# Half-height last passes, in pairs of tiles, in the first feed-forward contraction of an adaLN block

## The chip, the cores and the metric

The kernel runs on 1 core of one Trainium2 chip. The metric is device time in microseconds (us) of that core: a program's time from start to end, as the median of its runs. Beside it stands one profiled execution, from which every duration below is read.

## What is computed

One transformer block on 2048 tokens of width 448 with adaptive layer norm, in float32: sliding-window attention (16 heads, window 256), then a dense feed-forward part of width 1792 with the Mish activation. Cut to what matters here:

```python
mod = (silu(c) @ w_mod).reshape(1, 6, 1, -1)
sa, ca, ga, sb, cb, gb = (mod[:, i] for i in range(6))
h = layernorm(x) * (1 + ca) + sa
x = x + ga * attention(h, wqkv, wo)
h = layernorm(x) * (1 + cb) + sb
h = einsum("bsd,df->bsf", h, w1) + b1        # the first contraction: 448 -> 1792
act = h * tanh(softplus(h))                  # Mish
x = x + gb * einsum("bsf,fd->bsd", act, w2)  # the second contraction: 1792 -> 448
```

## The kernel before

Tokens are worked through in 4 groups g of 512. Every float32 matrix operand is split into a high and a low part, both of type float32r: a product is then high x high + high x low + low x high, three passes over each piece of 128 rows of the contraction. The contraction length 448 is three pieces of 128 rows and one of 64. For the piece of 64 the tiles hold the data twice, in rows 0 to 63 and again in rows 64 to 127: the activations' high and low parts (`hh`, `hl`) are doubled as they are, and of the weights (`w13[:, 3]`) rows 0 to 63 hold the high part and rows 64 to 127 the low part. So one pass of 128 rows gives high x high and high x low together, and a second one with `hl` gives low x high and, beside it, low x low, which is not needed. That makes 11 passes (`passes`, L183; low x high of the last piece is the eleventh). All of them are matmuls of 128 rows.

The feed-forward part has NF = 14 tiles f of 128 hidden features for each group, numbered through as n = 14 g + f, 0 to 55. For a tile n:

- `f1_mm(n)` (L812) puts 11 passes of 512 columns into one PSUM bank z (two such banks, taken in turn).
- `f1_act(n)` (L822): ACT makes Mish of z into `t` (L826, one buffer) and from it the high part `ah` (L827, two buffers); DVE takes the low part `al` (L828, two buffers) as the difference.
- `ff2(n)` (L992): 12 passes of 448 columns, three for each of the 4 token tiles t, added up over f in 4 PSUM banks `acc` (four buffers, so the next group takes the same four banks). At f = 13 DVE reads each bank (L1005, `yo`), adds the residual (L1008), and SP stores the result. The `yo` tiles have three buffers.

The order is written out by hand, and each engine works through its own queue in that order. The main loop (L1035) does, for n: `f1_mm(n)`, `f1_act(n)`, in the first group `pieces(n)` (L792: splits `w2` of tile n, ACT L789 and POOL L790, and for n below 6 two pieces of `w1`, L164 and L170 or L172), a `fill_step`, `ff2(n - 1)`, and one or two more `fill_step`s. So PE has alternating 11 passes z and 12 passes acc: while ACT and DVE work on tile n, PE does `ff2(n - 1)`. A fill step issues a bit of other work: in group 0 the end of the attention part for the last group (`ot`, `wo`), and in groups 0 to 2 the layer norm and the transposes (`trf`, L232, with `hT_hi` L239 on ACT and `hT_lo` L236 and L243 on DVE) for the next group.

Tiles 0 and 1 are done already at the end of the attention loop, by the table `TAIL` (L835): tile 0 in two parts, the load of the activation table for Mish, `f1_act(0)`, tile 1 in two parts, `f1_act(1)`. `ff2(0)` follows in the main loop.

`w1_lo` (L709, through `split_lo` L168) makes the weights' low parts, for the last piece as one operation on rows 64 to 127.

Of the kernel before, what the change touches and what calls it, by code (L numbers as in the profile page):

```python
# [8 lines left out]
F32 = mybir.dt.float32  # L9
# [3 lines left out]
ALU = mybir.AluOpType  # L13

S, D, F, H, DH, W = 2048, 448, 1792, 16, 28, 256
NG, GT = 4, 512
NF = F // 128
# [34 lines left out]
def adaln_block(ctx: ExitStack, tc: tile.TileContext, x, wqkv, wo, w1, b1, w2, c, w_mod, out):  # L52
    nc = tc.nc
    PE, ACT, DVE, POOL = nc.tensor, nc.scalar, nc.vector, nc.gpsimd
# [3 lines left out]
    def dma(o, i):  # L58
        nc.sync.dma_start(o, i)
# [25 lines left out]
    def bank(tag, bufs, name):  # L85
        return PS[0].tile([128, 512], F32, name=name, tag=tag, bufs=bufs)
# [81 lines left out]
    def split_lo(piece, hi, lo, ci, eng):  # L168
        if ci < 3:
            eng.tensor_tensor(lo, piece, hi.bitcast(F32), op=ALU.subtract)  # L170
        else:
            eng.tensor_tensor(hi[64:128], piece[64:128], hi[64:128].bitcast(F32), op=ALU.subtract)  # L172
# [10 lines left out]
    def passes(xh, xl, wh, wl):  # L183
        r = []
        for ci in range(3):
            r += [(xh[:, ci], wh[:, ci]), (xh[:, ci], wl[:, ci]), (xl[:, ci], wh[:, ci])]
        return r + [(xh[:, 3], wh[:, 3]), (xl[:, 3], wh[:, 3])]
# [191 lines left out]
    c0, c1 = QCOLS[0]  # L379
    for ci in range(4):  # L380
        hi = wq3[:, ci, c0:c1]
# [60 lines left out]
    def xr_tile(name):  # L442
        return mid.tile([128, 512], F32, name=name, tag="xr", bufs=3)
# [237 lines left out]
    FW = {}  # L681
    w2h, w2l, w2p, h2, x1 = {}, {}, {}, {}, {}
# [16 lines left out]
    w1p = {}  # L699
# [5 lines left out]
    def w1_hi(n):  # L705
        ci, c0 = W1[n]
        split_hi(w1p[n], FW["w13"][:, ci, c0:c0 + D], ACT)

    def w1_lo(n, eng):  # L709
        ci, c0 = W1[n]  # L710
        split_lo(w1p[n], FW["w13"][:, ci, c0:c0 + D], FW["w1l"][:, min(ci, 2), c0:c0 + D], ci, eng)


    SEQ = [e for f in range(NF) for e in [("w2", f)] + [("w1", n) for n in (2 * f + 4, 2 * f + 5) if n < len(W1)]]
# [1 line left out]
    def piece_load(i):  # L716
        if i < len(SEQ):
            (w2_dma if SEQ[i][0] == "w2" else w1_load)(SEQ[i][1])

    def gen_w1():  # L720
# [23 lines left out]
        for n in range(4):  # L744
            yield
            w1_hi(n)
            yield "dve"
            w1_lo(n, DVE)
# [34 lines left out]
    def w2_split(f):  # L783
        n = NF - 1 - f
        pl = FW["p1"] if f == 0 else FW["ff"]
        w2h[f] = (mid.tile([128, D], F32R, name=f"w2h{f}", tag="wo", bufs=7) if n < 7 else
                  pl.tile([128, D], F32R, name=f"w2h{f}"))
        w2l[f] = pl.tile([128, D], F32R, name=f"w2l{f}")
        ACT.activation(w2h[f], w2p[f], AF.Copy)  # L789
        (DVE if f < 1 else POOL).tensor_tensor(w2l[f], w2p[f], w2h[f].bitcast(F32), op=ALU.subtract)  # L790

    def pieces(f):  # L792
        for i, (kind, n) in enumerate(SEQ):
            if kind == "w2" and n == f:
                w2_split(n)
            elif kind == "w1" and (n - 4) // 2 == f:
                w1_hi(n)
                w1_lo(n, DVE if f < 1 else POOL)
            else:
                continue  # L800
            if "ff" in FW:
                piece_load(i + 6)

    NN = NG * NF
    ah, al, acc = {}, {}, {}

    def ftile(nm, n, dt=F32):
        return FW["p1"].tile([128, GT], dt, name=f"{nm}{n}", tag=nm, bufs=1 if nm == "t" else 2)

    zb = {}  # L810

    def f1_mm(n, tag, part=(0, 11)):  # L812
        g, f = divmod(n, NF)
        hh, hl = h2[g]
        fs = slice(f * 128, (f + 1) * 128)
        if part[0] == 0:
            zb[n] = bank(tag, 2, f"z{n}")
        ps = passes(hh, hl, FW["w13"][:, :, fs], FW["w1l"][:, :, fs])
        for m in range(*part):
            PE.matmul(zb[n], ps[m][1], ps[m][0], start=(m == 0), stop=(m == 10))  # L820

    def f1_act(n):  # L822
        f = n % NF
        ah[n], al[n] = ftile("ah", n, F32R), ftile("al", n, F32R)
        t = ftile("t", n)
        ACT.activation(t, zb[n], AF.Mish, bias=FW["b1c"][:, f:f + 1])  # L826
        ACT.activation(ah[n], t, AF.Copy)  # L827
        DVE.tensor_tensor(al[n], t, ah[n].bitcast(F32), op=ALU.subtract)  # L828

    def mish_table():  # L830
        ACT.add_instruction(mybir.InstLoadActFuncSet(
            act_func_set_id=25, name=nc.get_next_instruction_name(),
            engine=mybir.EngineType.Activation, ins=[], outs=[]))

    TAIL = {  # L835
        0: lambda: (f1_mm(0, "mm", (0, 6)), pieces(0)),
        1: lambda: (f1_mm(0, "mm", (6, 11)), mish_table(), f1_act(0)),
        2: lambda: f1_mm(1, "mm", (0, 6)),
        3: lambda: (f1_mm(1, "mm", (6, 11)), f1_act(1)),
    }  # L840

    VT = ("v0", "v1", "v2", "v3")
# [87 lines left out]
    for u in range(NU + 9):  # L930
        s, k = divmod(u, 3)
        g = s // H
# [12 lines left out]
        a = s + LEAD  # L945
# [46 lines left out]
    def ff2(n):  # L992
        g, f = divmod(n, NF)
        if f == 0:
            acc[g] = [bank("acc", 4, f"acc{g}_{t}") for t in range(4)]
        for t in range(4):
            ts = slice(t * 128, (t + 1) * 128)
            p = acc[g][t][:, 0:D]
            PE.matmul(p, ah[n][:, ts], w2h[f], start=(f == 0), stop=False)  # L999
            PE.matmul(p, ah[n][:, ts], w2l[f], start=False, stop=False)  # L1000
            PE.matmul(p, al[n][:, ts], w2h[f], start=False, stop=(f == NF - 1))  # L1001
            if f == NF - 1:
                j = 4 * g + t
                y = xr_tile(f"yo{j}")[:, 0:D]
                DVE.tensor_tensor(y, p, gbn, op=ALU.mult)  # L1005
                for eng, a, b in (((DVE, 0, D),) if g < NG - 1 else ((POOL, 0, D),) if t < 3 else
                                  ((DVE, 0, 256), (POOL, 256, D))):
                    eng.tensor_tensor(y[:, a:b], y[:, a:b], x1[g][:, t, a:b], op=ALU.add)  # L1008
                dma(of[j * 128:(j + 1) * 128, :], y)

    def gen_x1_ln2(g):
        if g > 1:
            x1_load(g, (ff, p1)[g % 2])
            yield
            yield
            yield

        def xn_tiles():
            t = mid.tile([128, 4, 512], F32, name=f"xn2_{g}", tag="on")
            return [t[:, i] for i in range(4)]  # L1020
        yield from gen_ln2(g, ff, xn_tiles, "tr", 2)
# [8 lines left out]
    def fill_step():  # L1030
        if fill is not None:
            pipe.step()
            next(fill, None)
            flush()
    for n in range(NN + 1):  # L1035
        g, f = divmod(n, NF)
        if f == 0 and n:
            while fill is not None and next(fill, "END") != "END":
                pipe.step()
            fill = None  # L1040
            while pipe.items:
                pipe.step()
        if f == 2 and 0 < g < NG - 1:
            fill = gen_x1_ln2(g + 1)
        if 2 <= n < NN:
            f1_mm(n, "z")
            f1_act(n)
        if 0 < n < NF:
            pieces(n)
        if n:  # L1050
            fill_step()
            ff2(n - 1)
            for _ in range(1 + (g == 0)):
                fill_step()
    for st in (ff_s, mid_s, cst_s, FW["s"], psf_s):
# [24 lines left out]
```

## Time and profile before

| what | value |
| --- | --- |
| runs, median of 3 | 728.78 us (727.68 to 729.99) |
| profiled execution, span from its first to its last instruction | 727.2 us |
| PE matmul busy | 690.9 us, 95% of the span, 3969 instructions |
| VectorE (DVE) busy | 381.4 us, 52% |
| ScalarE (ACT) busy | 392.3 us, 54% |
| GpSimd (POOL) busy | 331.2 us, 46% |
| granted TensorE clock, mean | 0.989 |
| first contraction, matmuls z (L820) | 224 + 224 + 168 |
| second contraction, matmuls acc (L999 to L1001) | 224 each |

The profile gives no time of the profiled execution beside its span; the span is 1.6 us below the median of the runs. The feed-forward part runs from about 422 us to the end. A matmul's duration in the records is from its start to its modelled end; matmuls overlap in the engine, so what a pass costs a full queue is the distance from its start to the next one's start. PEld are the weight loads, which normally run beside the matmul ahead of them. In a row of the timeline stand start, duration, engine, line, operation, output <- inputs, and in brackets how long the engine sat idle before it and what ended that.

### The profile page before, as it was taken

The page shows a single profiled execution, that of the slowest core. Times are in us where ns is not written, and L with a number is a line of the kernel's source. Part 1 is how long each engine was busy: PE and PEld are TensorE (multiplying, and loading weights), DVE is VectorE, ACT ScalarE, POOL GpSimd, SP SyncE. Part 2 cuts the span into 40 slices and gives each one's busy share as a digit, 9 for nine tenths or more (in the row PEclk, how much of TensorE's full clock was granted, in tenths as well). Part 3 has the DMA queues.
Part 4 walks back from the last instruction along what each step waited for, and adds up shares of the span by engine and source line. Part 5 has one row for each costly group of instructions (what it writes and reads, how often), then busy time and mean ns, then how long its engine had stood idle before and what let it go on. Part 6 is the DMA issues. An engine that isn't in the chain of part 4 may idle for free.

```text
span 727.2 us, 11903 instructions
## 1 busy us (share of the span) xinstructions
PE 690.9 (95%) x3969; PEld 588.4 (81%) x3969; DVE 381.4 (52%) x1011; ACT 392.3 (54%) x740; POOL 331.2 (46%) x362
## 2 busy tenths in 40 slices
PE   3989989999999999999999899999999999999996
PEld 2767768888889888888887688888888888888885
DVE  4768645687765688655668942334333223322112
ACT  3516777676776667766878984344223222322221
POOL 4725697676666586766778955322010000000002
PEclk9898999999999999999999999999999999999999
DMA  8776564174483354471666175300300020001001
GB/s 201 213 239 190 186 200 135 56 234 130 123 260 132 115 173 147 137 217 56 182 202 191 48 239 166 115 13 1 102 0 1 1 101 1 1 1 51 1 0 51
DMA packets 48121, 83.86 MB, mean 115 GB/s; under 512 B 6126, under 2 KB 26108, under 8 KB 48060
## 3 DMA queue, kind: packets, MB, share of 16 engines
q1 hardware_dynamic: 48060, 83.10, 37.6%
q8 instruction: 32, 0.52, 0.3%
q14 instruction: 29, 0.24, 0.1%
HBM read 53.45 MB, written 29.36 MB: 114 GB/s over the span
## 4 chain that ended last, share of the span: by engine, by line
PE 69%; issue 11%; DVE 8%; ACT 5%; DMA 4%; POOL 2%; SPq 1%; POOLq 0%; DVEq 0%; ACTq 0%
PE z L820 15%; PE pv L642 8%; PE qk L294 7%; PE qk_v L294 5%; PE acc L1000 5%; PE acc L1001 5%; PE acc L999 5%; PE sA L580 4%; PE wo L294 4%; PE sB L610 4%; PE sB L621 3%; DVE junk L582 3%; ACT P L624 2%; PE et L653 1%; DMA wm<-in_w_mod_dram 1%
## 5 line engine op out<-in xcount | busy, mean ns | idle before, releaser
L632 POOL TENSOR_TENSOR Pl<-P,Ph 128x512 fp32r<-128x512 f32 (+2 forms) x192 | 232.9, 1221 | 80.9 <-ACT Ph L625 47.8
L582 DVE CUSTOM_DVE_ANT_0 junk<-sA,mask 128x384 f32<-128x384 f32 (+2 forms) x256 | 135.3, 529 | 100.7 <-PE sA L580 95.4
L828 DVE TENSOR_TENSOR al<-t,ah 128x512 fp32r<-128x512 f32 x56 | 38.8, 692 | 200.9 <-ACT ah L827 200.9
L624 ACT ACTIVATE P<-sB 128x512 f32<-128x512 f32 (+2 forms) x192 | 109.7, 571 | 63.0 <-PE sB L621 56.2
L826 ACT ACTIVATE t<-z,b1c 128x512 f32<-128x512 f32 x56 | 38.5, 688 | 188.6 <-PE z L820 177.7
L625 ACT ACTIVATE Ph<-sB 128x512 fp32r<-128x512 f32 (+2 forms) x192 | 109.3, 569 | 0.0
L580 PE MATMUL sA<-k,q 84*128 84x384 f32 (+2 forms) x256 | 101.0, 399 | 5.7 <-DVE mx L582 5.2
L820 PE MATMUL z<-hhf,w 128*128 128x512 f32 x224 | 89.5, 400 | 0.0
L820 PE MATMUL z<-hlf,w 128*128 128x512 f32 x224 | 88.8, 396 | 0.0
L999 PE MATMUL acc<-w2h,ah 128*128 128x448 f32 x224 | 82.1, 367 | 0.0
L1000 PE MATMUL acc<-w2l,ah 128*128 128x448 f32 x224 | 82.1, 367 | 0.0
L1001 PE MATMUL acc<-w2h,al 128*128 128x448 f32 x224 | 82.0, 366 | 0.0
L642 PE MATMUL pv<-Pl,v 128*60 128x256 f32 (+2 forms) x352 | 74.2, 285 | 5.1 <-POOL Pl L632 5.0
L642 PE MATMUL pv<-Ph,v 128*60 128x256 f32 (+2 forms) x352 | 76.9, 292 | 2.2 <-ACT o L647 2.0
L610 PE MATMUL sB<-q,k 86*128 86x256 f32 (+1 forms) x352 | 75.1, 287 | 0.4 <-DMA q<-mr 0.2
L820 PE MATMUL z<-hhf,w1l 128*128 128x512 f32 x168 | 66.3, 395 | 0.0
L610 PEld LDWEIGHTS sB<-q,k 86*128 86x128 f32 x352 | 62.2, 191 | 2.3 <-DMA q<-mr 0.6
L621 PE MATMUL sB<-fdmask,identr 128*128 128x128 bf16 (+1 forms) x320 | 60.5, 255 | 0.0
L580 PEld LDWEIGHTS sA<-k,q 84*128 84x128 f32 x256 | 49.3, 194 | 12.9 <-DVE mx L582 11.1
L642 PEld LDWEIGHTS pv<-Ph,v 128*60 128x60 f32 x352 | 45.5, 133 | 16.4 <-ACT o L647 4.3
L642 PEld LDWEIGHTS pv<-Pl,v 128*60 128x60 f32 x352 | 44.9, 132 | 16.2 <-POOL Pl L632 9.6
L1008 POOL TENSOR_TENSOR yo<-yo,x 128x448 f32<-128x448 f32 (+1 forms) x4 | 4.2, 1060 | 108.6 <-DVE yo L1005 108.6
(150 smaller groups left out, 1290.6 us busy)
## 6 DMA issues: line engine op xcount, KB each, us to landing
scr<-st SPq DMA_DIRECT2D x24, 512.0 KB
k<-scr SPq DMA_DIRECT2D x48, 252.0 KB
q<-scr SPq DMA_DIRECT2D x64, 168.0 KB
scr<-st SPq DMA_DIRECT2D x32, 256.0 KB
x<-x1d SPq DMA_DIRECT2D x10, 448.0 KB
xin<-in_A_x_dram SPq DMA_DIRECT2D x8, 448.0 KB
xr<-in_A_x_dram SPq DMA_DIRECT2D x16, 224.0 KB
x1d<-xr SPq DMA_DIRECT2D x16, 224.0 KB
```

Of the source, the lines that this page charges most:

```text
L294: PE.matmul(p, b, a, start=(n == 0), stop=(n == 10))
L580: PE.matmul(p[:, c0:384], q[0:84, t * 128:(t + 1) * 128], k[0:84, t * 128 + c0:t * 128 + 384], start=True, stop=True)
L582: DVE.tensor_tensor_reduce(out=junk[:, c0:384], in0=p[:, c0:384], in1=mask[:, c0:384], scale=1.0, scalar=-3.0e38, op0=ALU.add, op1=ALU.max ...
L610: PE.matmul(p[:, c:c + 128 * (t1 - t0)], k[:, jj * 128:(jj + 1) * 128], q[:, t0 * 128:t1 * 128], start=(n == 0), stop=False, skip_group_ch ...
L624: ACT.activation(P[:, c0:], p[:, c0:], AF.Exp, scale=SCALE)
L625: ACT.activation(Ph[u][:, c0:], p[:, c0:], AF.Exp, scale=SCALE)
L632: eng.tensor_tensor(Pl[u][:, a:b], Pt[u][:, a:b], Ph[u][:, a:b].bitcast(F32), op=ALU.subtract)
L642: PE.matmul(pv[0:60, t0 * 128:t1 * 128], V[j % NV][:, h, :], P[u][:, c:c + 128 * (t1 - t0)], start=(P is Ph and b == 0 and n == 0), stop=F ...
L820: PE.matmul(zb[n], ps[m][1], ps[m][0], start=(m == 0), stop=(m == 10))
L999: PE.matmul(p, ah[n][:, ts], w2h[f], start=(f == 0), stop=False)
L1000: PE.matmul(p, ah[n][:, ts], w2l[f], start=False, stop=False)
L1001: PE.matmul(p, al[n][:, ts], w2h[f], start=False, stop=(f == NF - 1))
```

## The change

The last pass of each z tile (low x high of the 64-row piece) becomes a matmul of 64 rows: rows 0 to 63 for even f, rows 64 to 127 for odd f. So that an odd tile finds the weights' high part in rows 64 to 127, `w1_lo` now puts the low part into rows 0 to 63 for odd f, in pieces of at most 128 columns: four operations in place of one for each of the four last-piece blocks of `w1`.

Tiles go in pairs (n even): ten passes for n, ten for n + 1, then both half-height passes one behind the other (`f1_end`), then `f1_act(n)`. `f1_act(n + 1)` comes behind `ff2(n - 1)`. At odd n the loop now holds `pieces(n)`, fill steps and `ff2(n - 1)` alone. In `TAIL` tile 0 is no longer finished by itself: both halves and both `f1_act` stand at its end.

```diff
     def w1_lo(n, eng):
         ci, c0 = W1[n]
-        split_lo(w1p[n], FW["w13"][:, ci, c0:c0 + D], FW["w1l"][:, min(ci, 2), c0:c0 + D], ci, eng)
+        if ci < 3:
+            split_lo(w1p[n], FW["w13"][:, ci, c0:c0 + D], FW["w1l"][:, ci, c0:c0 + D], ci, eng)
+            return
+        a = c0
+        while a < c0 + D:
+            f = a // 128
+            b = min((f + 1) * 128, c0 + D)
+            r = slice(64, 128) if f % 2 == 0 else slice(0, 64)
+            hi = FW["w13"][r, 3, a:b]
+            eng.tensor_tensor(hi, w1p[n][r, a - c0:b - c0], hi.bitcast(F32), op=ALU.subtract)
+            a = b
...
-    def f1_mm(n, tag, part=(0, 11)):
+    def f1_mm(n, tag, part=(0, 10)):
...
-            PE.matmul(zb[n], ps[m][1], ps[m][0], start=(m == 0), stop=(m == 10))
+            PE.matmul(zb[n], ps[m][1], ps[m][0], start=(m == 0), stop=False)
+
+    def f1_end(n):
+        for i in (n, n + 1):
+            g, f = divmod(i, NF)
+            r = slice(64 * (f % 2), 64 * (f % 2) + 64)
+            PE.matmul(zb[i], FW["w13"][r, 3, f * 128:(f + 1) * 128], h2[g][1][r, 3], start=False, stop=True)
...
     TAIL = {
-        0: lambda: (f1_mm(0, "mm", (0, 6)), pieces(0)),
-        1: lambda: (f1_mm(0, "mm", (6, 11)), mish_table(), f1_act(0)),
-        2: lambda: f1_mm(1, "mm", (0, 6)),
-        3: lambda: (f1_mm(1, "mm", (6, 11)), f1_act(1)),
+        0: lambda: (f1_mm(0, "mm", (0, 5)), pieces(0)),
+        1: lambda: (f1_mm(0, "mm", (5, 10)), mish_table()),
+        2: lambda: f1_mm(1, "mm", (0, 5)),
+        3: lambda: (f1_mm(1, "mm", (5, 10)), f1_end(0), f1_act(0), f1_act(1)),
     }
...
-        if 2 <= n < NN:
+        if 2 <= n < NN and n % 2 == 0:
             f1_mm(n, "z")
+            f1_mm(n + 1, "z")
+            f1_end(n)
             f1_act(n)
         if 0 < n < NF:
             pieces(n)
         if n:
             fill_step()
             ff2(n - 1)
+            if 2 <= n < NN and n % 2 == 0:
+                f1_act(n + 1)
```

Three places show what moves. PE, the end of tile 14's z passes and the start of `ff2(13)`, before (`hhf1`, `hlf1` are the high and low part of group 1's input, `w13` the weights' high part, `ah13` and `al13` the parts of tile 13's activations):

```order
L820 MATMUL z14_6791<-hhf1_6587,w1l_5223 128x512
L820 MATMUL z14_6791<-hlf1_6588,w13_5222 128x512
L820 MATMUL z14_6791<-hhf1_6587,w13_5222 128x512
L820 MATMUL z14_6791<-hlf1_6588,w13_5222 128x512
L999 MATMUL acc0_0_6180<-w2h13_6773,ah13_6767 128x448
```

and the same place in the change:

```order
L830 MATMUL z15_6814<-hlf1_6618,w13_5222 128x512
L830 MATMUL z15_6814<-hhf1_6617,w13_5222 128x512
L836 MATMUL z14_6803<-hlf1_6618,w13_5222 128x512
L836 MATMUL z15_6814<-hlf1_6618,w13_5222 128x512
L1015 MATMUL acc0_0_6186<-w2h13_6785,ah13_6773 128x448
```

Ahead of `ff2(13)` now stand both tiles 14 and 15, and the two half-height passes (L836) follow each other between a pass of 128 rows and the next pass of 128 rows.

PE, a little further, where group 0's last `ff2` ends and group 1's first begins, before (`acc0_3` is the fourth accumulator of group 0, `acc1_0` the first of group 1, in the bank that `acc0_0` had):

```order
L999 MATMUL acc0_3_6183<-w2h13_6773,ah13_6767 128x448
L1000 MATMUL acc0_3_6183<-w2l13_6774,ah13_6767 128x448
L1001 MATMUL acc0_3_6183<-w2h13_6773,al13_6768 128x448
L820 MATMUL z15_6837<-hhf1_6587,w13_5222 128x512
L820 MATMUL z15_6837<-hhf1_6587,w1l_5223 128x512
L820 MATMUL z15_6837<-hlf1_6588,w13_5222 128x512
```

and in the change:

```order
L1015 MATMUL acc0_3_6189<-w2h13_6785,ah13_6773 128x448
L1016 MATMUL acc0_3_6189<-w2l13_6786,ah13_6773 128x448
L1017 MATMUL acc0_3_6189<-w2h13_6785,al13_6774 128x448
L1015 MATMUL acc1_0_6867<-w2h0_6067,ah14_6827 128x448
L1016 MATMUL acc1_0_6867<-w2l0_6068,ah14_6827 128x448
L1017 MATMUL acc1_0_6867<-w2h0_6067,al14_6828 128x448
```

The 11 passes of z15 that stood between the two `ff2` are gone from there. DVE's queue at this place holds `al14`, then the four pairs of `yo` operations, then `al15`, before and now.

ACT, at the end of the attention loop, before (`o2_1` is the last head's output out of PSUM, `ol31` a step of the last pair of heads):

```order
L831 ACT_TABLE_LOAD
L826 ACTIVATE t0_6089<-z0_6058,b1c_5469 128x512
L827 ACTIVATE ah0_6087<-t0_6089 128x512
L647 ACTIVATE o2_1_367<-pv63_6048 60x512
L826 ACTIVATE t1_6112<-z1_6098,b1c_5469 128x512
L827 ACTIVATE ah1_6110<-t1_6112 128x512
L658 ACTIVATE ol31_6121<-et31_6116 128x224
```

and in the change:

```order
L847 ACT_TABLE_LOAD
L647 ACTIVATE o2_1_367<-pv63_6051 60x512
L842 ACTIVATE t0_6109<-z0_6061,b1c_5469 128x512
L843 ACTIVATE ah0_6107<-t0_6109 128x512
L842 ACTIVATE t1_6115<-z1_6094,b1c_5469 128x512
L843 ACTIVATE ah1_6113<-t1_6115 128x512
L658 ACTIVATE ol31_6124<-et31_6119 128x224
```

Tile 0's activation now stands behind the last head's output and directly ahead of tile 1's.

## Prediction

> **What bounds the kernel now.** First the page, then the stretches of the feed-forward part, then single rows.
>
> ```profile
> PE 690.9 (95%) x3969; PEld 588.4 (81%) x3969; DVE 381.4 (52%) x1011; ACT 392.3 (54%) x740; POOL 331.2 (46%) x362
> ```
>
> ```profile
> 600.00:650.00 50.00, 50.00 (x239) 43.17 (x238) 14.40 (x22) 14.55 (x22) 1.14 (x4) 1.00 0.00 1
> ```
>
> The second line is a stretch of 50 us in the feed-forward part: PE (first figure behind the length) is busy for all 50.00, DVE and ACT for 14.4 and 14.55, at full granted clock. Here PE alone sets the time, and a pass less in its queue is worth the distance from one pass to the next. Rows of PE in that stretch, for one tile:
>
> ```profile
> 600.72 0.39 PE L820 MATMUL z<-hhf,w 128*128 128x512 f32 x1
> ...
> 603.05 0.40 PE L820 MATMUL z<-hlf,w 128*128 128x512 f32 x1
> 603.29 0.37 PE L999 MATMUL acc<-w2h,ah 128*128 128x448 f32 x1
> ...
> 605.77 0.39 PE L820 MATMUL z<-hhf,w 128*128 128x512 f32 x1
> ```
>
> The first row is the first of 11 passes z, the second the last: ten steps take 2.33 us, a pass 0.233 us (not the 0.39 of its record). The 12 passes acc take 605.77 - 603.29 = 2.48 us, 0.207 each. Durations come from one execution with a span of 727.2 us; the median of the runs, 728.78, lies 1.6 above it. What the change adds inside the span is added to the median.
>
> **The two half-height passes.** There are 28 pairs. Before, their two passes cost 2 x 0.233 = 0.466 us. If both halves run at once and nothing else happens, a pair saves 0.233, in all 6.5 us: the end below nothing. What speaks for more than that is how PE changes between shapes of tile. One kind of change the trace has hundreds of times, to fewer columns (128*60 in the rows) and back:
>
> ```profile
> 300.22 0.39 PE L294 MATMUL qk<-hh,wql 128*128 128x512 f32 x1
> 300.45 0.40 PE L642 MATMUL pv<-Ph,v 128*60 128x256 f32 x2
> 300.68 0.40 PE L642 MATMUL pv<-Pl,v 128*60 128x256 f32 x2
> 300.92 0.40 PE L610 MATMUL sB<-q,k 86*128 86x256 f32 x2
> ```
>
> The starts lie 0.23 apart throughout, 512 columns each: changing columns costs nothing. Fewer rows occur once, in the transpose b1t with 14 rows (L741):
>
> ```profile
> 384.12 0.18 DVE L193 BATCH_NORM_AGGREGATE mv<-stw 128x2 f32<-128x6 f32 x1
> 384.27 0.36 PE L294 MATMUL wo<-wo,hho 128*128 128x448 f32 x1
> 384.56 0.13 PEld L741 LDWEIGHTS b1t<-ident,b1r 14*128 14x128 f32 x1 [0.31 <-DVE mv L193]
> 384.72 0.18 PEld L642 LDWEIGHTS pv<-Ph,v 128*60 128x60 f32 x2
> 385.00 0.40 PE L642 MATMUL pv<-Pl,v 128*60 128x256 f32 x2
> ```
>
> Its weight load waits for DVE, which ends at 384.30, and starts 0.26 later. What a wait for DVE costs otherwise shows an ordinary load of 128 rows:
>
> ```profile
> 243.94 0.69 DVE L317 TENSOR_TENSOR st<-qk,st 128x512 fp32r<-128x512 f32 x1
> 244.69 0.19 PEld L294 LDWEIGHTS qk<-hh,wq 128*128 128x128 f32 x1 [0.59 <-DVE st L317]
> 244.79 0.19 PEld L294 LDWEIGHTS qk<-hh,wql 128*128 128x128 f32 x1
> 245.03 0.40 PE L294 MATMUL qk<-hh,wql 128*128 128x512 f32 x1
> ```
>
> DVE ends at 244.63, the load starts 0.06 later. So b1t's load is held 0.20 longer, until 0.08 after the pass of wo has run out (384.27 + 0.207 = 384.48). And a load that nothing hides costs 0.10: the next one starts 0.10 behind it, and the two passes lie 0.34 apart in place of 0.23. Behind b1t, the first of the two pv(Ph) passes must have begun 0.23 before 385.00, at 384.77. From the end of wo's pass to there are 0.29 us, for a pass of 14 columns: that is the round trip into fewer rows and back.
>
> The pair in the same way: 0.29 for the round trip, 0.05 more because the load behind it has 128 columns and not 60 (an estimate, half of the 0.10), 0.10 for the second half's own load, 0.23 for the columns of both at once: 0.67 against 0.466, so +0.20 a pair and +5.7 us for 28. Upper end: the halves run one after the other, 0.29 + 0.05 + 0.47 = 0.81, +9.6 us. I take +5.7 because b1t is the only row with fewer rows, and its load visibly did not start beside the pass ahead of it.
>
> [...]
>
> **The new order at the change of groups.** ff2(14) takes the four accumulator banks of ff2(13). Before, the 11 passes of z15 stand between them; now ff2(14) follows at once. This is what DVE does with the banks (tiles 41 and 42, the same place in a later group):
>
> ```profile
> 649.85 0.40 PE L820 MATMUL z<-hlf,w 128*128 128x512 f32 x1
> 650.09 0.36 PE L999 MATMUL acc<-w2h,ah 128*128 128x448 f32 x1
> 650.28 0.69 ACT L826 ACTIVATE t<-z,b1c 128x512 f32<-128x512 f32 x1 [3.64 <-PE z L820]
> 651.67 0.69 DVE L828 TENSOR_TENSOR al<-t,ah 128x512 fp32r<-128x512 f32 x1 [4.30 <-ACT ah L827]
> 652.28 0.62 DVE L1005 TENSOR_TENSOR yo<-acc,gbn 128x448 f32<-128x448 f32 x1
> ...
> 655.86 0.62 DVE L1005 TENSOR_TENSOR yo<-acc,gbn 128x448 f32<-128x448 f32 x1
> ```
>
> Call M the start of Mish, 650.28, which lies 0.43 behind the last z pass. DVE must do al first, so the first of four yo starts at M + 2.00, and the fourth frees its bank at 656.48, M + 6.20. PE can load for that bank 0.06 later, exposed 0.10, and needs 3 x 0.207 for it: ff2(14) ends at M + 6.98. Left to itself it would end earlier: of the pair's 0.67, 0.18 lie ahead of the first half's start (0.08 + 0.10) and 0.49 behind it, so acc starts at M - 0.43 + 0.49 = M + 0.06, and 24 passes end at M + 5.03. PE waits 1.95 us, at each of the three changes of group: +5.9 us. Before, 2.56 us of z15 covered this: M - 0.19 + 4.97 + 2.56 = M + 7.34. That cover is what moved. ACT and DVE are not held by more than PE; stores and loads on SP follow DVE as before.
>
> **The start.** Tiles 0 and 1:
>
> ```profile
> 428.16 0.69 ACT L826 ACTIVATE t<-z,b1c 128x512 f32<-128x512 f32 x1 [0.68 <-PE z L820]
> 428.74 0.45 PE L999 MATMUL acc<-w2h,ah 128*128 128x448 f32 x1
> 428.88 0.63 ACT L827 ACTIVATE ah<-t 128x512 fp32r<-128x512 f32 x1
> 429.43 0.37 PE L999 MATMUL acc<-w2h,ah 128*128 128x448 f32 x1
> 429.54 0.69 DVE L828 TENSOR_TENSOR al<-t,ah 128x512 fp32r<-128x512 f32 x1 [1.96 <-ACT ah L827]
> ```
>
> These are tile 1's Mish, copy and al, while ff2(0) runs, whose inputs were ready. Now tile 0 has this place, and tile 1 comes behind it, since t has one buffer: its Mish waits for al(0), M + 2.07. ff2(0)'s fourth pass takes a bank of the attention part that tile 1's Mish still reads (M + 2.1 to 2.8): with 0.06 and 0.10 it starts at M + 2.95. M itself is 0.05 earlier (one pass ahead of it fewer by 0.23, 0.18 of switch), 428.11, so 431.06 against 429.43 + 0.20: +1.4 us. The last head's two steps on ACT behind it are late by about as much, and PE does not wait for them: z2 and z3 stand between.
>
> **Smaller waits.** In group 0, ff2(n) for even n needs w2l(n), which POOL makes behind ACT's copy; ff2(n - 1) alone now stands between z and it:
>
> ```profile
> 474.63 0.69 ACT L826 ACTIVATE t<-z,b1c 128x512 f32<-128x512 f32 x1 [3.22 <-PE z L820]
> 476.53 1.19 POOL L790 TENSOR_TENSOR w2l<-w2p,w2h 128x448 fp32r<-128x448 f32 x1 [3.08 <-ACT w2h L789]
> ```
>
> That is tile 8: w2l is ready at M + 3.09, and with 0.06 usable at 3.15; PE wants it at M + 0.06 + 2.48 + 0.21 = M + 2.75: 0.4 and an exposed load, +0.5. In tiles 10 and 12 four transposes stand between:
>
> ```profile
> 482.04 0.44 PE trf L232 x4
> ```
>
> They cover it. The layer norm for the next group loses cover too, in groups 1 and 2, where the fourth set of transposes needs a bank that DVE empties:
>
> ```profile
> 548.74 0.76 ACT L239 ACTIVATE hhf<-trf,cols 128x512 fp32r<-128x512 f32 x1
> 549.53 0.82 DVE L236 TENSOR_SCALAR trf<-trf,cols 128x512 f32<-128x512 f32 x1
> 550.38 0.69 DVE L243 TENSOR_TENSOR hlf<-trf,hhf 128x512 fp32r<-128x512 f32 x1
> ```
>
> Its DVE steps (1.54) now stand behind al of the odd tile: copy of the even tile ends at M + 1.35, then 0.77 of L239, Mish 0.72, copy 0.63, al 0.7, 1.54: M + 5.7, with 0.06 M + 5.77, where PE comes at M + 0.06 + 2 x 2.48 + 0.44 = M + 5.46. +0.3, twice: +0.6.
>
> At nothing: the four short operations in place of one in w1_lo. POOL and DVE have time there, and the pieces are made two and more tiles ahead; only for tile 3 is that one tile, and there PE's wait at the start gives 1.4 us of cover. Without it z3 would wait once, for less than a us.
>
> Sum: 5.7 + 5.9 + 1.4 + 0.5 + 0.6 = 14.1 us. 728.8 + 14.1 = 742.9 us (span 741.3).
>
> **Rivals.** First, no switch price: both halves start together behind the pass ahead. For it: the pv rows. Against: b1t. Then -6.5; but acc starts at M - 0.19, 0.25 sooner against M, so every wait grows: three changes at 2.2, the start 1.7, w2l 0.75 and twice 0.3, transposes twice 0.55: 10.8 in all less 6.5, 733.1 us. [...]
>
> Second, the halves take their turn like any passes, no switch and no overlap: the pair costs 0.466 as before, the waits stay as in the forecast, 8.4 us: 737.2.
>
> Third, the other side: the halves overlap for nothing, and the change of groups does not hold PE, because the banks come free in time. Place: the four L1005 at three changes. Then -6.5 + 1.7 + 1.35 + 1.1 = -2.4: 726.4 us. It decides when a change holds PE for less than 0.8 us. For it: before, PE never waits there. Against: DVE's queue is unchanged and its rows fix M + 6.20, which PE reaches 2 us early.
>
> **How the numbers follow.** Forecast 0.60, first rival 0.22, second 0.10, third 0.05; 0.03 for something else. A measurement of this kernel can tell about 0.3% from no change, 2.2 us: 726.6 to 731.0. The third rival gives faster 0.05; same takes 0.06, from the first rival with waits 2.3 us smaller and from the rest; slower 0.89. The range reaches down to the first rival, 732.5, and up by the pair's upper end (+3.9) and some for waits that add up, 748.5.
>
> **What would show it.** Right: L836's weight load starts after the pass ahead has run out, not beside it, and from the last z of 128 rows to acc there are some 0.9 us (0.23 + 0.67); PE idle of about 2 us, in three or four pieces and ended by DVE yo, at each change of group; 1.4 us at the start, ended by ACT; Mish, al and yo as long as before. Wrong: the two L836 start within 0.02 us of each other and of the pass's slot (first rival), 0.23 apart with no gap (second), or no PE idle at 14, 28 and 42 (third).

## The result, and the profile after

| | before | changed |
|---|---|---|
| median of 6 runs each, us | 729.38 | 748.34 |
| lowest to highest | 727.68 to 732.24 | 745.63 to 750.02 |
| span of the profiled execution | 727.2 | 747.3 |

The ratio is 1.0241, with a 95% interval of 1.0224 to 1.0259: on 729.4 us that is 17.6 us more, 16.3 to 18.9. The two medians of the table lie 19.0 apart. Differences in time below are worked out from such ratios, unless they are said to be of a trace. The forecast was +14.1 and the range reached to 748.5, so the measured median lies only 0.2 us inside it. The sum came out too low, by errors that in part offset each other. The profile says which.

First the page's line of busy times, of the changed kernel.

```profile
PE 702.1 (94%) x3969; PEld 582.8 (78%) x3969; DVE 383.2 (51%) x1014; ACT 391.2 (52%) x740; POOL 332.6 (45%) x371
```

The count of PE's instructions is the same, and its busy time is 11.2 us longer: a record of a half-height pass (0.49 in place of 0.40) or of a pass of acc that started late (0.47 in place of 0.37) is longer, which is no more work. DVE has three instructions more and POOL nine: the pieces of `w1_lo`. The places where the time lies have to be read from PE's timeline.

**A pair.** Rows of PE and of its weight loads (PEld) at one pair in the middle of the feed-forward part:

```profile
550.39 0.40 PE L830 MATMUL z<-hhf,w 128*128 128x512 f32 x1
550.72 0.49 PE L836 MATMUL z<-hlf,w 64*128 64x512 f32 x2
551.14 0.47 PE L1015 MATMUL acc<-w2h,ah 128*128 128x448 f32 x1
551.45 0.37 PE L1016 MATMUL acc<-w2l,ah 128*128 128x448 f32 x1
```

```profile
550.72 0.19 PEld L836 LDWEIGHTS z<-hlf,w 64*128 64x128 f32 x2 [0.36 <-issue]
551.14 0.19 PEld L1015 LDWEIGHTS acc<-w2h,ah 128*128 128x128 f32 x1 [0.24 <-issue]
```

The last pass of 128 rows starts at 550.39 and would be through its slot of 0.233 at 550.62. The loads of both halves start at 550.72, 0.09 behind that. The two half-height passes stand in one row with a length of 0.49, the record of one alone: in the trace the second starts 3 ns behind the first. The pass of acc follows at 551.14 and the one behind it 0.31 later in place of 0.207. From 550.39 to 551.45 are 1.06 us, and without the two slots around the pair 1.06 - 0.233 - 0.207 = 0.62 is left, against 0.466 before: +0.156 a pair, taken from the unrounded starts, and 28 times that is 4.4 us.

**A change of groups.** PE around the first bank of group 1, then DVE at the same place:

```profile
520.86 0.37 PE L1017 MATMUL acc<-w2h,al 128*128 128x448 f32 x1
521.38 0.44 PE L1015 MATMUL acc<-w2h,ah 128*128 128x448 f32 x1 [0.15 <-DVE yo L1021]
...
522.49 0.47 PE L1015 MATMUL acc<-w2h,ah 128*128 128x448 f32 x1 [0.25 <-DVE yo L1021]
...
523.68 0.47 PE L1015 MATMUL acc<-w2h,ah 128*128 128x448 f32 x1 [0.32 <-DVE yo L1021]
...
524.87 0.47 PE L1015 MATMUL acc<-w2h,ah 128*128 128x448 f32 x1 [0.32 <-DVE yo L1021]
```

```profile
520.01 0.69 DVE L844 TENSOR_TENSOR al<-t,ah 128x512 fp32r<-128x512 f32 x1 [6.35 <-PE acc L1017]
520.62 0.62 DVE L1021 TENSOR_TENSOR yo<-acc,gbn 128x448 f32<-128x448 f32 x1
521.27 0.63 DVE L1024 TENSOR_TENSOR yo<-yo,x 128x448 f32<-128x448 f32 x1
521.82 0.62 DVE L1021 TENSOR_TENSOR yo<-acc,gbn 128x448 f32<-128x448 f32 x1
```

Each bank comes free 1.2 us behind the one before, when DVE's yo has read it, and PE's three passes a bank take 0.62: it stands four times. By the distances of the starts, with each exposed load, it loses 0.39 + 0.51 + 0.58 + 0.58 = 2.05 us, and the like at 596 and at 672 us.

**The start.** Tile 0's `ff2`, where ACT's steps come late:

```profile
435.06 0.47 PE L1015 MATMUL acc<-w2h,ah 128*128 128x448 f32 x1 [0.42 <-ACT ah L843]
435.37 0.37 PE L1016 MATMUL acc<-w2l,ah 128*128 128x448 f32 x1
435.78 0.47 PE L1017 MATMUL acc<-w2h,al 128*128 128x448 f32 x1
436.56 0.47 PE L1015 MATMUL acc<-w2h,ah 128*128 128x448 f32 x1 [0.31 <-ACT t L842]
```

PE waits for the copy ah, then for al, then for tile 1's Mish, which still reads the bank: 1.57 us with the exposed loads.

**Before the feed-forward part.** The first z starts at 427.4 in the changed kernel and at 421.9 before, 5.5 us apart, although the change adds nothing to PE there. Rows of PE, DVE and GpSimd (POOL) in the last part of the attention:

```profile
409.11 0.68 PE L580 MATMUL sA<-k,q 84*128 84x384 f32 x1 [1.94 <-DVE mx L582]
```

```profile
405.49 3.09 DVE L720 TENSOR_TENSOR w<-w1p,w 64x128 fp32r<-64x128 f32 x4
408.51 0.54 DVE L582 CUSTOM_DVE_ANT_0 junk<-sA,mask 128x384 f32<-128x384 f32 x1
```

```profile
405.84 2.67 POOL L632 TENSOR_TENSOR Pl<-P,Ph 128x512 fp32r<-128x512 f32 x2
```

and the same operation of DVE in the kernel before, where it was one:

```profile
404.10 0.62 DVE L172 TENSOR_TENSOR w<-w1p,w 64x448 fp32r<-64x448 f32 x1
```

DVE's four short operations take 3.09 us and not 0.62. The maximum behind them (L582) comes late, and PE waits 1.94 us for it. After that wait PE is also slower, as the granted clock shows (0.66, the figure behind POOL's busy time and count, against 1.00 in the same stretch before):

```profile
409.00:414.00 5.00, 4.89 (x28) 4.39 (x29) 4.79 (x15) 2.53 (x5) 2.56 (x3) 0.66 0.00 0
```

Laid against the kernel before pass by pass, PE is 1.4 us late before 400 us, by two DMA waits that are longer by 0.5 and 0.9 in this execution. The wait for the maximum and the lower clock behind it add 2.4. The last 1.7 us come from a second stretch at a lower clock, just ahead of the first z:

```profile
422.50:426.50 4.00, 3.83 (x18) 3.44 (x19) 2.23 (x4) 2.96 (x7) 3.37 (x4) 0.57 0.50 146
```

That `w1_lo` causes this second stretch is not shown: of the runs below, same_rows with the old `w1_lo` has one at the same place (0.53 from 421.4 to 425.0), and split_only with the short operations has none there. From the first z to the end are 305.3 us before and 319.8 after: +14.6.

### The profile page after: what moved, and what is told of

It reads as the page before. It is cut to its first block, busy times and chain, and to the rows that moved or that the text cites. A ratio compares the mean times of both kernels' runs of the same rounds, so it can differ in the third digit from the quotient of the medians.

```text
span 747.3 us, 11938 instructions
## 1 busy us (share of the span) xinstructions
PE 702.1 (94%) x3969; PEld 582.8 (78%) x3969; DVE 383.2 (51%) x1014; ACT 391.2 (52%) x740; POOL 332.6 (45%) x371
## 4 chain that ended last, share of the span: by engine, by line
PE 59%; issue 11%; DVE 11%; DMA 9%; ACT 5%; SPq 3%; POOL 1%; POOLq 0%; DVEq 0%; ACTq 0%
PE z L830 14%; PE pv L642 7%; PE qk L294 5%; PE acc L1015 4%; PE sA L580 4%; PE acc L1016 4%; PE acc L1017 4%; PE wo L294 4%; PE sB L610 3%; PE qk_v L294 3%; DVE junk L582 3%; SPq L59 3%; DMA k<-scr 2%; PE sB L621 2%; DMA xin<-in_A_x_dram 2%
## 5 line engine op out<-in xcount | busy, mean ns | idle before, releaser
L582 DVE CUSTOM_DVE_ANT_0 junk<-sA,mask 128x384 f32<-128x384 f32 (+2 forms) x256 | 135.2, 528 | 101.5 <-PE sA L580 96.3
L1015 PE MATMUL acc<-w2h,ah 128*128 128x448 f32 x224 | 86.7, 387 | 3.9 <-DVE yo L1021 3.2
L830 PE MATMUL z<-hhf,w 128*128 128x512 f32 x224 | 84.8, 398 | 0.0
L830 PE MATMUL z<-hlf,w 128*128 128x512 f32 x168 | 66.4, 395 | 0.0
L1015 PEld LDWEIGHTS acc<-w2h,ah 128*128 128x128 f32 x224 | 42.1, 188 | 17.7 <-issue 7.6
```

Source lines behind the costliest of these rows:

```text
L582: DVE.tensor_tensor_reduce(out=junk[:, c0:384], in0=p[:, c0:384], in1=mask[:, c0:384], scale=1.0, scalar=-3.0e38, op0=ALU.add, op1=ALU.max ...
L830: PE.matmul(zb[n], ps[m][1], ps[m][0], start=(m == 0), stop=False)
```

## The experiments

Theory: the 17.6 us are three things that add up, the order (waits where PE's cover went), the pairs (a switch into half-height rows and back, less the overlap of the halves), and `w1_lo`'s short operations. Rivals: the halves do not overlap at all and the switch is nearly free; or the order costs nothing and the halves cost everything; or `w1_lo` is innocent and the late start of z is chance.

**The order alone** (order_only): the kernel before, with the new order and both tiles' last passes at full height.

```diff
...
+    def f1_end(n):
+        for i in (n, n + 1):
+            g, f = divmod(i, NF)
+            r = slice(0, 128)
+            PE.matmul(zb[i], FW["w13"][r, 3, f * 128:(f + 1) * 128], h2[g][1][r, 3], start=False, stop=True)
...
```

> The pairs and their order as in the change, but both last passes with all 128 rows and w1_lo as before: no change of row mode, no overlap, no short DVE operations. Theory (the new order itself costs about 11 us in waits of PE, the switches about 4): slower than before by 8 to 11 us, some 738 to 740, with PE waiting 2.0 us at each change of group, 1.5 us at the start, 1 us or less in each of the other places. Rival (the loss is the switching and the waits are its consequence): within 2 us of before.

Measured: 739.27 us, ratio 1.013 (1.0105 to 1.0156), +9.5 us. Its waits are those of the change: 1.5 us at the start, 2.03 at each change of groups, 0.8 with its load in group 0's last projection (wo), 0.5 twice at the transposes, 0.6 at tile 8 and 0.2 each at tiles 10 and 12 for `w2l`. Its trace is 9.4 us longer from the first z on. The order alone costs about half of the whole (by the intervals, 7.7 to 11.4 of 17.6).

**Half height alone** (halves_only): the order of before, each tile's last pass with rows 0 to 63, so 56 times into half height and back with no partner.

```diff
-            PE.matmul(zb[n], ps[m][1], ps[m][0], start=(m == 0), stop=(m == 10))
+            r = slice(0, 64 if m == 10 else 128)
+            PE.matmul(zb[n], ps[m][1][r], ps[m][0][r], start=(m == 0), stop=(m == 10))
```

> The kernel before in its own order; only the last pass of each tile has 64 rows (always rows 0 to 63), so there are 56 changes into fewer rows and back and nothing runs beside them. Theory (each round trip costs 0.39 us beside the columns, as the trace of the change shows it): slower by 56 x 0.39 = 22 us, about 751, spread evenly over the tiles. Rival (what the change lost is the order alone, a pass of 64 rows costs as much as one of 128): within 2 us of before.

Rows of PE at one tile:

```profile
600.85 0.39 PE L821 MATMUL z<-hhf,w 128*128 128x512 f32 x1
601.16 0.50 PE L821 MATMUL z<-hlf,w 64*128 64x512 f32 x1
601.59 0.47 PE L1000 MATMUL acc<-w2h,ah 128*128 128x448 f32 x1
601.90 0.37 PE L1001 MATMUL acc<-w2l,ah 128*128 128x448 f32 x1
```

Measured: 750.18 us, ratio 1.0267 (1.0243 to 1.0292), +19.5 us or 0.35 a tile. The rows give 0.31 + 0.43 + 0.31 where three slots of full height give 0.233 + 0.233 + 0.207: 0.38 a round trip, and 0.39 is the median of the tiles. 56 times that is 21.7 us; the 2.2 us between this and the measured time are not assigned. These rows can be laid beside those of the pair in the change, and hardly differ (1.05 and 1.06 us): in the pair the second half adds nothing.

**Both halves in the same rows** (same_rows): the change, with both half-height passes in rows 0 to 63 and with the old `w1_lo`.

```diff
...
-            r = slice(64 * (f % 2), 64 * (f % 2) + 64)
+            r = slice(0, 64)
...
```

> The change with both halves of a pair in rows 0 to 63, and w1_lo as before. Theory (in the change the two halves run at once, 3 ns apart): here the second starts 0.21 to 0.23 us behind the first, 28 x 0.22 = 6 us more than the change, less some 3 us because the short operations of w1_lo are gone: 750 to 753. Rival (the halves did not overlap in the change, the records only start together): as the change without the short operations, 744 to 746.

The pair and what stands around it:

```profile
549.98 0.40 PE L820 MATMUL z<-hhf,w 128*128 128x512 f32 x1
550.30 0.74 PE L826 MATMUL z<-hlf,w 64*128 64x512 f32 x2
550.97 0.47 PE L1005 MATMUL acc<-w2h,ah 128*128 128x448 f32 x1
551.28 0.37 PE L1006 MATMUL acc<-w2l,ah 128*128 128x448 f32 x1
```

Measured: 750.28 us, ratio 1.0275 (1.0252 to 1.0298). The two passes last 0.74 together in place of 0.49, and the same four rows take 1.30 us and not 1.06: the overlap of the halves in the change is worth 0.233 a pair, one whole pass. So a pair costs one round trip (0.39) less one overlap (0.233), +0.156. By these figures it would need a second overlap in the same trip to gain, which no run here tried. From the first z on, the trace is 4.2 us longer than the change's and not 28 x 0.233 = 6.5, since PE waits less behind a longer pair: the two waits of 0.5 us at the transposes are gone, and a change of groups holds it for 1.8 us in place of 2.05.

**`w1_lo`'s pieces alone** (split_only): the kernel before, the last chunk's subtraction in four operations, all in rows 64 to 127, so that the computation is the same.

```diff
...
+        while a < c0 + D:
+            f = a // 128
+            b = min((f + 1) * 128, c0 + D)
+            r = slice(64, 128)
+            hi = FW["w13"][r, 3, a:b]
+            eng.tensor_tensor(hi, w1p[n][r, a - c0:b - c0], hi.bitcast(F32), op=ALU.subtract)
+            a = b
...
```

> The kernel before, with w1_lo's last piece made in four operations of at most 128 columns, all in rows 64 to 127 as before. Theory (the four operations on DVE in the attention part wait for GpSimd one by one and hold up the score maxima and so PE): slower by 2 to 4 us, and the four DVE operations take about 3 us together in place of 0.62. Rival (the 2 us at that place in the profile of the change are chance): within 1 us of before.

Measured: 733.71 us, ratio 1.0052 (1.0033 to 1.007), +3.8 us, with nothing of the order or the height changed. The same place on DVE and on POOL:

```profile
404.83 3.04 DVE L720 TENSOR_TENSOR w<-w1p,w 64x128 fp32r<-64x128 f32 x4
```

```profile
404.90 0.31 POOL L196 COPY x<-x 128x64 f32<-128x64 f32 x1
405.17 2.61 POOL L632 TENSOR_TENSOR Pl<-P,Ph 128x512 fp32r<-128x512 f32 x2
```

The four take 0.29, 0.33, 1.37 and 1.29 us. (The fourth has 64 columns, the others 128.) The third starts at 405.28, behind the start of the first of POOL's two multiplications, and ends at 406.66, 0.15 behind its end; the fourth ends 0.08 behind the end of the second. The first two lie beside the short copy. PE then waits 2.02 us for the maximum, 2.3 us are lost there against the kernel before, and about 1 us more in a stretch at a lower clock behind it (0.50 from 410.4 to 413.8). From the first z on the trace is as long as before, 305.3 us.

**Two operations in place of four** (split_two): split_only, with DVE's piece in two of 224 columns; POOL's pieces stay in four.

```diff
...
-            b = min((f + 1) * 128, c0 + D)
+            b = min((f + 1) * 128 if eng is POOL else a + 224, c0 + D)
...
```

> As split_only, which cost 3.7 us, but DVE's piece is done in two operations of 64x224 and not in four of 64x128; GpSimd's pieces stay in four. In split_only the first two took 0.29 and 0.33 us and ended before or with GpSimd's short copy; the third and fourth took 1.37 and 1.29 and each ended 0.09 to 0.16 us behind a multiplication of GpSimd (L632) that had begun before it. Theory (DVE's two-input operation stands aside until the GpSimd operation that began first has ended, so the number of operations that fall beside L632 sets the cost): both fall ahead of the first L632, the piece takes 0.6 to 0.8 us in all, mx is not late, and the time is within 0.3% of the kernel before, ratio 1.000. Rival (short operations are slow of themselves, or GpSimd's split pieces are what costs): two operations still take 2 us or more, or the cost stays although they take 0.7, ratio 1.003 to 1.005.

```profile
403.75 0.73 DVE L720 TENSOR_TENSOR w<-w1p,w 64x224 fp32r<-64x224 f32 x2
```

Measured: 730.24 us, ratio 0.9999 (0.9983 to 1.0014). Two operations take 0.73 us; the second starts at 404.06, ahead of POOL's next multiplication at 404.20. So it is not POOL's pieces, and splitting in itself costs little; the time goes with how many of DVE's operations come to stand behind nearly the whole of a multiplication of POOL's: none here, one in pool_add4 below (2.11 us), two in split_only (3.04) and in the change (3.09). The third and fourth operation of split_only started behind a multiplication and ended 0.15 and 0.08 us after it; in the change they took 1.28 and 1.20 us and ended 0.15 and 0.08 after one. The first operation here (from 403.75) has only the last 0.12 us of a multiplication ahead of it (to 403.87), and the one operation of the kernel before (404.10 to 404.72) the last 0.13 (to 404.23), where the next begins at 404.78. What holds DVE back there no trace shows.

**The old order at the change of groups** (old_at_change): the change, but tiles 0 and 1 of groups 1 to 3 one at a time and at full height.

```diff
...
-        if 2 <= n < NN and n % 2 == 0:
+        if NF <= n < NN and f < 2:
+            f1_mm(n, "z")
+            f1_end(n, 1)
+            f1_act(n)
+        elif 2 <= n < NN and n % 2 == 0:
...
```

> This is the change, but the first two tiles of groups 1, 2 and 3 are worked through in the old order, one tile at a time, with last passes of full height; the other 25 pairs stay as they are. Theory (PE waits at a change of groups because the order no longer puts a tile's passes between the two accumulations that share the four banks): the waits at 520, 596 and 672 us go, 3 x 2.05 = 6.15 us, and three pairs less pay 0.156 each, 0.5 us; together 6.6 us under the change, near 741.7 us, ratio to the kernel before near 1.016, and no PE idle ended by DVE yo in the three places. Rival (the four banks pass the delay on: what is not waited for at the change is waited for at the next pair): waits of about 2 us turn up one or two tiles later, and the time stays within 1.5 us of the change, near 748, ratio near 1.024.

Measured: 741.27 us, ratio 1.0168 (1.0116 to 1.022), against 1.0241 for the change: 5.3 us less by the ratios, 7.5 by the spans (739.8 against 747.3); its four runs spread widely, from 739.3 to 746.4. The three waits are gone and come back nowhere:

```profile
517.45 0.37 PE L1017 MATMUL acc<-w2h,al 128*128 128x448 f32 x1
517.66 0.40 PE L830 MATMUL z<-hhf,w 128*128 128x512 f32 x1
```

That is where group 0's last `ff2` ends: the next pass follows 0.21 later. The spans differ by 0.9 more than the 6.6 expected, and this execution has no wait at wo, which in the change's is 0.9 us with its load.

**DVE's part of that wait** (pool_add): the change, with the addition behind every yo on GpSimd.

```diff
-                for eng, a, b in (((DVE, 0, D),) if g < NG - 1 else ((POOL, 0, D),) if t < 3 else
+                for eng, a, b in (((POOL, 0, D),) if g < NG - 1 or t < 3 else
...
```

> This is the change with its order and its pairs, but the addition of the residual behind every yo (out of shared memory into shared memory, four for each group) runs on GpSimd in all groups and not on DVE. Theory (the wait at a change of groups is DVE's queue: al, then four times yo and an addition, 1.2 us a bank): with 0.62 us a bank the fourth bank comes free about 1.7 us sooner, each wait of 2.05 us shrinks to about 0.4, and the time falls by 4.5 to 5 us, to near 743.5, ratio to the kernel before near 1.019. Rival (the wait is set by the arrival of ACT's copy and al, not by the additions between the yo): the waits stay near 2 us, and the time near 748, ratio near 1.024. A second rival: GpSimd's additions lengthen the DVE operations beside them, as in the stretch near 406 us, and yo takes about 1.2 us itself; then nothing is won either, but yo's own duration shows it.

Measured: 753.97 us, ratio 1.0331 (1.0289 to 1.0373), slower still, which neither expectation had. DVE at the first change of groups:

```profile
517.07 1.68 DVE L1021 TENSOR_TENSOR yo<-acc,gbn 128x448 f32<-128x448 f32 x3
521.01 0.62 DVE L1021 TENSOR_TENSOR yo<-acc,gbn 128x448 f32<-128x448 f32 x1 [2.26 <-DMA out_dram<-yo]
```

Three yo now follow each other 0.53 apart, but the fourth needs the buffer of the first (there are three), and waits until GpSimd has added to it and a DMA has stored it. PE's waits in small pieces became one of 0.31 and one of 1.92 us, with an exposed load behind each, and at the third change the long one is 3.25. Behind the first long wait the clock falls:

```profile
522.50:526.00 3.50, 3.50 (x11) 2.65 (x10) 0.00 (x0) 0.00 (x0) 1.97 (x3) 0.54 0.43 109
```

In this window eight steps from pass to pass of z take 0.43 in place of 0.233. It falls again behind the third (0.50 from 676.4 to 679.8), but not behind the second, where PE waits 1.96 us:

```profile
599.00:602.50 3.50, 3.28 (x15) 2.76 (x16) 0.77 (x2) 0.00 (x0) 2.76 (x3) 1.00 0.49 147
```

The experiment tested the buffer and not the theory.

**With a fourth buffer** (pool_add4): the same, with four places for yo.

```diff
-        return mid.tile([128, 512], F32, name=name, tag="xr", bufs=3)
+        return mid.tile([128, 448], F32, name=name, tag="xr", bufs=4)
```

> As pool_add (the additions behind yo on GpSimd), and yo's buffer has four places (of 448 columns) and not three, so that the fourth yo waits for no store. In pool_add the first three banks came free at 0.56 us apart, and the first pieces of the wait were gone (0.31 left of some 1.1), but the fourth yo stood 2.26 us for the store of the first, behind GpSimd's additions of 1.1 us. Theory (DVE's queue sets the wait, and only the store put itself in its place): now the fourth bank follows 0.6 us behind the third, the wait at a change of groups is 0.3 to 0.5 us in all against 2.05, three times, and the time is 4.5 to 5 us under that of the change, near 743.5, ratio to the kernel before near 1.019. Rival: something else still holds the fourth bank (GpSimd's additions, which would lengthen yo; or al), with 1.5 us or more left at each change and a ratio near 1.024.

DVE and PE at the first change of groups:

```profile
517.91 2.21 DVE L1021 TENSOR_TENSOR yo<-acc,gbn 128x448 f32<-128x448 f32 x4
```

```profile
518.14 0.37 PE L1017 MATMUL acc<-w2h,al 128*128 128x448 f32 x1
518.67 0.44 PE L1015 MATMUL acc<-w2h,ah 128*128 128x448 f32 x1 [0.17 <-DVE yo L1021]
518.95 0.36 PE L1016 MATMUL acc<-w2l,ah 128*128 128x448 f32 x1
519.15 0.36 PE L1017 MATMUL acc<-w2h,al 128*128 128x448 f32 x1
519.35 0.37 PE L1015 MATMUL acc<-w2h,ah 128*128 128x448 f32 x1
```

Measured: 741.25 us, ratio 1.015 (1.0128 to 1.0171). All four yo run in one go, PE waits once, 0.33 and 0.07 of exposed load, at all three changes: 1.65 us less each, 5.0 in all. By the ratio the kernel is 6.6 us faster than the change, more than the 4.5 to 5 expected. From the first z on its trace is 5.6 us shorter than the change's. Its first z stands at 424.7, 2.7 us earlier; 1.5 of these were there before 400 us, and in the rest of the attention only one of DVE's short `w1_lo` operations stood behind POOL, so that the piece took 2.11 us. That part has nothing to do with this edit.

None of these beats the kernel before. By the rows of the pair 4.4 us would be left even without any wait, since the round trip costs more (0.39) than the overlap gives back (0.233).

## Why the prediction was right, and where it was not

The parts add up: the order 9.5 and `w1_lo` 3.8 from runs of their own, the pairs 28 x 0.156 = 4.4 from the rows of the change, together 17.7 us, where the ratio gives 17.6. That the two agree to a tenth is luck, as the intervals are 7.7 to 11.4 for the order and 2.4 to 5.1 for `w1_lo`. The direction, the switch and the waits were forecast; the size was not, as the total fell at the very top of the range because one cost was put at nothing and several waits were too small.

**The pair: mechanism right, size a little high.** The load of the half-height pass does start after the pass ahead has run out (0.09 behind it), as b1t's row had it (0.08). The term was 0.67 and is 0.62, so +4.4 and not +5.7. The part that fell away is the 0.10 for the second half's own load, which runs beside the first one's; the round trip itself is a little dearer than the 0.34 taken from b1t (0.39). The prediction called b1t the only row with fewer rows than 128. That was a misreading: its own row of sB has 86, and 608 passes of the attention have 84 or 86 rows and cost no switch (a pass of 256 columns ahead of one of 86 rows takes 0.118 us, as ahead of one of 128, and one of 512 columns ahead of one of 84 rows 0.233). What costs here is the change to 64 rows, or b1t's 14, and b1t was the right model all the same. The first rival was half right: the halves do start together, 3 ns apart. What this rival lacked was the switch, and the traces now have its price, 0.39 us a round trip. That the columns of both run at once, 0.23 in the sum, no row of before shows; the rows of the change do, and in same_rows, where they go in turn, the pair takes 0.233 more. The second rival, halves in turn and no switch, came about nowhere: in same_rows they do go in turn, but pay the switch too (0.86 a pair, not 0.466).

**The change of groups: right.** 1.95 was forecast and 2.05 measured, in four pieces ended by yo, because DVE's queue, al and then 1.2 us a bank, sets the time of the fourth bank. Undoing the order removes it and shortening DVE's queue leaves 0.40 of it, so the third rival's condition (less than 0.8 us) was not met.

**The start: right**, 1.57 for 1.4, and its cause is ACT's order.

**The smaller waits: too small.** Tile 8's w2l is 0.58 for 0.5; tiles 10 and 12, put at nothing under four transposes, wait 0.23 each; the transposes of the next layer norm wait 0.5 and not 0.3. One wait was not seen at all, 0.9 us with its load in group 0's last projection:

```profile
462.97 0.48 PE L294 MATMUL wo<-wo,hho 128*128 128x448 f32 x1 [0.63 <-DVE xr L533]
```

```profile
460.67 1.71 DVE L844 TENSOR_TENSOR al<-t,ah 128x512 fp32r<-128x512 f32 x1 [2.09 <-ACT ah L843]
```

Here al takes 1.71 us and not 0.69, beside a subtraction of POOL (two of L170, 459.56 to 461.83), and ends 0.55 behind it; no run changed this al alone, so the cause of its length is not shown. The other traces fit: in the four of the new order in which it takes 1.4 us or more, PE waits at wo, and in old_at_change and pool_add, where it does not, PE does not wait.

**The step that failed: the four short operations "at nothing".** The prediction asked whether POOL and DVE have time, and whether the piece is made early enough for its reader. It did not ask what DVE's own queue delays: the maximum behind it, on which PE waits at once. And it gave the four short operations no duration, where DVE's took 3.09 us and one had taken 0.62. They cost 3.8 us by split_only; in the trace of the change it is 2.4 at that place, with the lower clock behind the wait. This was the largest single error. The smaller waits were 1.8 us too low together, and the pair, taken 1.3 us too high, covered a part.

**What stays open.** Behind the first z the rows' terms give 4.4 + 6.15 + 1.6 + 1.0 + 1.0 + 0.9 = 15.1 us, and the stretches differ by 14.6; before it the spans differ by 5.5, without the DMA waits 4.1. That is 18.7 by the two profiled executions, 19.0 by the medians and 17.6 by the ratio. What lies between them is not assigned; runs of the changed kernel differ by up to 4.4 us. Open too is what brings the second stretch of lower clock, 1.7 of these 4.1 us.

## What to carry to other kernels

Splitting one operation into several short ones was not free here: DVE's four took 3.04 us beside POOL's multiplications (split_only), where one had taken 0.62 (before) and two took 0.73 (split_two). Count the operations that can come to stand behind the neighbour's, and look at what is next in the engine's own queue. Half-height passes did not pay here with one overlap to a switch of height: the switch costs 0.39 us and each overlapped pass gives back 0.233, so by an estimate from these two figures it takes two or more, which was not tried. Work that stands between the last use of a buffer and its next use is cover, and a reordering that groups like with like spends it, here at 2.05 us a change of groups.

## What had not been expected of the hardware

- The loads of two half-height passes in different rows also run together (3 to 4 ns apart in the change), and so do the passes; in the same rows the second starts 0.34 behind the first, and the pair takes 0.233 more (same_rows).
- A change of height from 128 to 64 rows costs a round trip of 0.39 us (halves_only): 0.09 ahead of the half, 0.19 behind its columns, 0.10 at the first pass of acc, whose next load nothing hides; the changes of width (128 to 60 columns), and to 84 or 86 rows, in the attention part cost nothing (0.118 for 256 columns and 0.233 for 512 ahead of such a pass, as elsewhere).
- DVE's operation of 64x128 takes 0.28 us where it starts ahead of a multiplication of GpSimd's (the change) and up to 1.37 behind one, ending 0.15 us after it (split_only).
- A long wait of PE's can cost more than its length: in pool_add, behind one of 1.92 us, the granted clock was 0.54 over the next 3.5 us. But behind one of 1.96 us in the same trace it stayed at 1.00, so the length alone does not decide. Four waits of 0.4 to 0.6 us with passes between them, at the three changes of groups of the change, left the passes of z behind them at 0.233 and a granted clock of 1.00.
